# When a weight load is issued around a branch: attention, cosine routing and eight experts on one core

## The chip, the cores and the metric

The kernel runs on one core of a Trainium2 chip. A core has TensorE (PE, with PEld for its weight loads), VectorE (DVE), ScalarE (ACT), GpSimd (POOL) and SyncE (SP), each with its own stream of instructions; they meet through semaphores. Transfers are issued from the streams of SP and POOL and run on 16 DMA engines, which also bring the blocks of code that the engines execute. The metric is device microseconds of the core, median of three runs; lower is better.

## The reference

What is computed is an attention with a local window and a few global keys, and then a mixture of experts that gives each token to one expert:

```python
# attention: B=4, H=8, S=768, D=64; keys 0..7 and the last 96 are kept, with a bias by distance
a = exp(scores - max); a = a / (sum(a) + 1e-9); x = a @ v          # x: 3072 tokens of 512
# experts: E=8, F=1024
logits = unit(x) @ unit(expert_emb).T / tau
expert_idx = argmax(logits, axis=1)
gate_w = softmax(logits)[expert_idx]
for e in range(E):
    mask = expert_idx == e
    h = maximum(x[mask] @ w1[e], 0)
    out[mask] = gate_w[mask, None] * (h @ w2[e])
```

All is float32. The weights of one expert are two matrices of 2 MB.

## The kernel before

The first 200 us are the attention with the choice of expert; each token's row is written to DRAM and its number, row and gate go into a list by expert. The change lies in what follows: the loop over the eight experts at the end of the kernel's main function.

**How many tokens.** The number of tokens of an expert is known only on the chip. It is rounded up to a width of 128, 160, 192, ..., 512 (256 is the least from expert 1 on), and for every width there is an arm of code of its own. `tc.Switch` in `expert` lets TensorE, ScalarE and VectorE jump into the arm; each jumps for itself, and each jumps back to the common code behind the arms ("behind the choice") for itself. The register that names the arm is loaded by `take_width` (L1491, one load each on TensorE, ScalarE and VectorE) for the expert after the next, and `give_hint` (L1497) tells the engines' fetch of code which arm comes next. With this case's data the widths are 160, 320, 512, 320, 352, 384, 480 and 384.

**Inside an arm.** `first_by_seven` computes h of experts 1 to 7 as a 2x2 block product with seven products instead of eight (products at L1286). It needs sums of blocks of w1 and of x, made by VectorE ahead of time: `first_sums` (L1064 to L1067, tile fsum; two run in the arm of the expert before, two behind it) and `token_sums` (L1039 to L1042, tile xsum, split the same way). VectorE's additions of results are L1298, ScalarE's copies and relus L1312, L1317 and L1300. Then `part_in_arm` (L1232, eviction L1234) multiplies a last group of 64 rows, or 32, or both, by w2, and `second_in_arm` (L1219, eviction L1221) does whole tiles of 128 rows beyond the first 256. For width 320 there is one part of 64 rows and no tile; 352 has both parts; 480 both parts and a tile; 512 two tiles. Between products the next expert's rows are transposed (L1011) and copied (L1014).

**Behind the arm.** The first 256 rows go through class `Pair`, again a 2x2 block product of seven products (L1101), with four banks of PSUM. `begin` makes four of them: the first is copied by ScalarE (L1121, tile ptmp), the second is added to it by VectorE (L1105) and scaled by ScalarE (L1125), the third is added (L1105) and scaled (L1131), the fourth gives one part of y (L1112). `end` makes three more; the last of all waits until ScalarE has taken the product before it out of the same bank (L1144). What is left of the previous expert's pair (`unfinished`, L1112 or, behind expert 0, L1029) is done by VectorE first. In expert 0 the pair of another set of rows is finished by `end_apart`.

**What sets the order.** The order on TensorE, ScalarE, VectorE and POOL is that of the program text. In the common code behind the arm VectorE has: the width, the rest of y, two sums of x, two sums of w1, then the pair's additions. SP's stream in this part holds only loads of weights. `prepare(e + 1)` names POOL's gathers of rows (L985) and, from expert 2 on, `load_weights` for the next expert: w1 (L167), then w2 (L168), into the buffers that expert e - 1 used. Each load waits for the last reader of its buffer: for w1 these are TensorE's products in the arm and VectorE, for w2 the end of the pair. POOL scatters finished rows (L1238).

Of the kernel before, what the change touches and what calls it, by code (L numbers as in the profile page):

```python
# [12 lines left out]
ALU = mybir.AluOpType  # L13
# [7 lines left out]
P = 128  # L21
# [142 lines left out]

def load_weights(k, e, w):
    nc = k.nc
    nc.sync.dma_start(w[0][:], k.w1[e].rearrange("(c p) f -> p c f", p=P))  # L167
    nc.sync.dma_start(w[1][:], k.w2[e].rearrange("(f p) m -> p f m", p=P))  # L168


def load_weights_part(k, e, w, i):
# [822 lines left out]
def new_turned(k):  # L994
    return k.xtp.tile([P, k.NC, 2, CAP // 2], F32, name="xT", tag="xT")


def new_hidden(k):
    return k.hp.tile([P, k.NF, CAP], F32, name="hT", tag="hT")
# [7 lines left out]
def turn_row(k, rows, xT, j, copy):  # L1007

    ps = k.work.tile([P, k.NC, P], F32, name="work", tag="work")
    for c in range(k.NC):  # L1010
        k.nc.tensor.transpose(ps[:, c, :], rows[2][j][:, c * P : (c + 1) * P], k.ident[:])  # L1011
    half = P // 2
    for a in range(2):
        copy(out=xT[:, :, a, j * half : (j + 1) * half].rearrange("p c (q i) -> p c q i", i=LACE),  # L1014
             in_=laced(ps[:])[:, a])
# [30 lines left out]
def weight_sums(k, w2):  # L1046

    b = [[w2[:, 4 * i : 4 * i + 4, j * 256 : (j + 1) * 256] for j in range(2)] for i in range(2)]
    return right_sums(k, b, k.wsum)


def token_sums(k, xT):

    b = [[xT[:, 2 * i : 2 * i + 2, j] for j in range(2)] for i in range(2)]
    return right_sums(k, b, k.xsum, True)
# [20 lines left out]
def first_sums(k, w1):  # L1076
    return left_sums(k, first_weights(k, w1), k.fsum, True)


def hidden_sums(k, a):  # L1080
    return left_sums(k, a, k.hsum)


class Pair:
# [24 lines left out]

    def last(self, i, out, x, z):  # L1110

        self.k.nc.vector.scalar_tensor_tensor(out=out, in0=x, scalar=self.gate[i], in1=z, op0=ALU.mult, op1=ALU.add)  # L1112

    def scatter(self, i):
        return lambda: scatter_rows(self.k, self.y[i][:], self.ids[:, i, 1:2])

    def begin(self, split=False):
        nc, (t1, t2, t3, t4), (s1, s2, s3, s4) = self.k.nc, self.sums, self.left
        m = self.m = self.bank()
        self.product(m, self.a[0][0], self.b[0][0])  # L1120
        nc.scalar.copy(out=self.p1, in_=m)  # L1121
        n = self.bank()
        self.product(n, s2, t2)
        self.plus(self.u2, n, self.p1)
        nc.scalar.mul(self.u2g, self.u2, self.gate[0])  # L1125
        if split:
            self.fourth()
        n = self.bank()
        self.product(n, s3, t3)
        self.plus(self.u3, n, self.u2)  # L1130
        nc.scalar.mul(self.u3g, self.u3, self.gate[1])  # L1131
        n = self.bank()
        self.product(n, self.a[1][1], t4)
        self.last(1, self.part(1, 0), n, self.u3g)

    def fourth(self):
        self.product(self.m, self.a[0][1], self.b[1][0], True)
        self.k.nc.scalar.mul(self.part(0, 0), self.m, self.gate[0])
# [16 lines left out]
    def end_apart(self):  # L1155

        t1, (s1, s2, s3, s4) = self.sums[0], self.left
        n = self.bank()
        self.product(n, s1, t1)
        self.last(1, self.part(1, 1), n, self.u3g)  # L1160
        self.last(0, self.u3, n, self.u2g)
        n = self.bank()
        self.product(n, s4, self.b[1][1])
        self.last(0, self.part(0, 1), n, self.u3)
        return [self.scatter(0), self.scatter(1)]
# [49 lines left out]
def second_in_arm(k, t, hT, w2, j):  # L1215
    nc = k.nc
    ps = k.work.tile([P, k.DM], F32, name="work", tag="work")
    for i, f in enumerate(k.order):
        nc.tensor.matmul(ps[:], lhsT=hT[:, f, j * P : (j + 1) * P], rhs=w2[:, f, :],  # L1219
                         start=i == 0, stop=i == k.NF - 1)  # L1220
    nc.scalar.mul(t.y[:, j - 1, :], ps[:], t.rows[0][:, j, 2:3])  # L1221
# [27 lines left out]
def wait_for(k, i, others):  # L1249
    for x in others:  # L1250
        k.tc.add_manual_dep(i.ins, x.name,
                            mybir.DependencyInfo(mybir.DependencyClass.Sync, mybir.DependencyReason.DATA),
                            reason="it comes behind all of them")
# [75 lines left out]
def expert(k, now, coming, widths, unfinished):  # L1329


    tc = k.tc
    w1, w2 = now.w
    hT = new_hidden(k)
    if coming:
        coming.xT = new_turned(k)

    def between(f):
        at = {1: (0,), 2: (1,), 3: (2,), 4: (3,)} if now.e else {5: (0,), 6: (1, 2), 7: (3,)}
        for j in at.get(f, ()) if coming else ():  # L1340
            turn_row(k, coming.rows, coming.xT, j, k.nc.scalar.copy)

    a = [[hT[:, 4 * j : 4 * j + 4, i * P : (i + 1) * P] for j in range(2)] for i in range(2)]
    now.sums, spare = weight_sums(k, w2)
    left, making = hidden_sums(k, a)
    more, ahead = [], []
    if coming:
        coming.token_sums, more = token_sums(k, coming.xT)
        if now.e:
            coming.first_sums, ahead = first_sums(k, coming.w[0])  # L1350
    spare = [spare[:2], spare[2:], ahead[:1], ahead[1:2], more[:2], []]
    tiles = range(2 if now.e else 1, CAP // P)
    ps = None if now.e else k.work0.tile([P, k.DM], F32, name="work", tag="work")
    k.order = list(range(4, 8)) + list(range(4)) if now.e else list(range(8))
    steps = widths_of(now.e)
    for arm in tc.Switch(now.width.index, len(steps), hint=now.width.hint):
        w = steps[arm]
        if now.e:
            first_by_seven(k, now, hT, w, between, list(spare))
            for make in making:  # L1360
                make()
        else:
            first_by_eight(k, now.xT, w1, hT, w, between)
        for size in (64, 32):
            if w % (2 * size) >= size:
                part_in_arm(k, now, hT, w2, w // (2 * size) * 2 * size, size)
        for j in tiles:
            if j < w // P:
                second_in_arm(k, now, hT, w2, j)
        if ps:  # L1370
            second(k, ps, hT, w2, range(k.NF // 2))

    def scatters():
        for j in tiles:
            scatter_rows(k, now.y[:, j - 1, :], now.tile_ids[:, j : j + 1])
        for size in (64, 32):
            scatter_rows(k, now.y_part[size][:], now.parts[size][0], P // size)

    def choose_next():
        if coming:  # L1380
            give_hint(k, coming.e, widths[coming.e])
        if now.e + 2 < k.E:
            widths.append(take_width(k, now.e + 2))

    out = [scatters]
    if now.e:
        pair = Pair(k, now.rows, a, left, w2, now.sums)
        choose_next()
        out += unfinished.pop()()
        for make in more[2:] + ahead[2:]:  # L1390
            make()
        pair.begin()
        ps = k.work0.tile([P, k.DM], F32, name="work", tag="work")
        unfinished.append(pair.end(ps[:, 0:256]))
        out.append(pair.scatter(1))
    else:
        choose_next()
        out += unfinished.pop()()
        for make in more:
            make()  # L1400
        second(k, ps, hT, w2, range(k.NF // 2, k.NF))
        unfinished.append(lambda: end_second(k, now.rows, ps))
    return out


def widths_of(e):
    return WIDTHS[PAIR:] if e else WIDTHS
# [78 lines left out]
def take_width(k, e):  # L1486

    t = Net()
    n = len(widths_of(e))
    engines = ARMS if e else ARMS[:2]  # L1490
    v = k.nc.values_load(k.pick[0:1, e : e + 1], engines=engines, min_val=0, max_val=n - 1)  # L1491
    t.index, t.hint = {eng: v for eng in engines}, "expert%d" % e
    return t
# [74 lines left out]
def kernel(  # L1568
# [13 lines left out]
    n = Net()  # L1582
    n.tc, n.nc = tc, tc.nc
    nc = n.nc
# [24 lines left out]
    with ExitStack() as moe:  # L1609
# [43 lines left out]
        def prepare(e):  # L1653
            t = Net()
            t.e = e
            t.y, t.y_part = ys[e % 2]
            xgs, t.gathers = gather_rows(n, n.ids[:, e], n.xgp)
            t.rows = n.mt[:, e], n.ids[:, e], xgs
            if e < 2:
                t.w = n.w[e]  # L1660
            else:
                t.w = new_weights(n, (wp_a, n.wp_b)[e % 2])
                load_weights(n, e, t.w)
            return t

        with tc.manual_schedule(engines=ORDERED | set(ARMS) | {mybir.EngineType.Pool}):
# [20 lines left out]
            widths = [take_width(n, 0), take_width(n, 1)]  # L1687
            give_hint(n, 0, widths[0])
            pair = Pair(n, n.first.rows, a, left, n.w[0][1], sums)
# [10 lines left out]
            first, making = first_sums(n, n.w[1][0])  # L1700
# [3 lines left out]
            for e in range(n.E):  # L1704
                now, coming = coming, None
# [44 lines left out]
```

## Time and profile before

| What | us |
| --- | --- |
| Median of the three runs (530.98 to 533.39) | 532.84 |
| The profiled execution's own time | 532.6 |
| Its span, from the first to the last instruction | 530.9 |
| TensorE busy in the span | 502.7 |
| VectorE, ScalarE, POOL busy | 302.2, 197.5, 148.3 |
| From the first product of expert 1's arm to the end of expert 7's pair | 234.3 to 523.5 |

| Expert | Width | Arm and pair, us | w1 for the next expert but one issued at | w2 issued at |
| --- | --- | --- | --- | --- |
| 0 | 160 | 208.8 to 234.3 | 222.95 | 234.31 |
| 1 | 320 | 234.3 to 271.0 | 253.19 | 269.14 |
| 2 | 512 | 271.0 to 324.9 | 305.80 | 324.93 |
| 3 | 320 | 324.9 to 359.5 | 343.79 | 359.58 |
| 4 | 352 | 359.5 to 397.7 | 383.12 | 397.72 |
| 5 | 384 | 397.7 to 436.8 | 417.68 | 436.86 |
| 6 | 480 | 436.8 to 486.1 | none | none |
| 7 | 384 | 486.1 to 523.5 | none | none |

A line of the order of time gives the start in us, the length, the engine, the line of the kernel, the operation, the tiles, and in brackets the idle time before it with what ended it. "Issue" there means that the profile shows nothing that the engine waited for; fetching code is such a case. A line can stand for several instructions in a row. Matmul ends are modelled. Times of TensorE's and VectorE's jumps, of packets and of the clock are from records of the same trace.

### The profile page before, as it was taken

Reading aid. Unit: us, or ns where it says so; the run is one execution under the profiler, and the core shown is the slowest. Engines: PE = TensorE matmul, PEld = TensorE weight load, DVE = VectorE, ACT = ScalarE, POOL = GpSimd, SP = SyncE. Lnnn points to the kernel's source line nnn. Section 1 sums busy time; section 2 is a strip of 40 time slices with the busy share of each in tenths; the row PEclk is TensorE's granted clock in tenths of the full one; section 3 lists DMA queues with packets and bytes.
Section 4 is the critical chain, followed back from the end, with each engine's and each line's share of the span. In section 5 each row is a group of like instructions: output and inputs, shape, how many; then the busy total and the mean of one; then the engine's idle time right before and its main releaser. Section 6 shows DMA issues by size and latency. Waiting matters only on the chain.

```text
span 530.9 us, 13718 instructions
## 1 busy us (share of the span) xinstructions
PE 502.7 (95%) x5606; PEld 412.8 (78%) x5606; DVE 302.2 (57%) x601; ACT 197.5 (37%) x494; POOL 148.3 (28%) x169
## 2 busy tenths in 40 slices
PE   8999999999989998999979999989999999999994
PEld 7677787877766687779758669979789789869963
DVE  5756767756686664848535624745646554733531
ACT  4966766766644311304022312312312222312210
POOL 4221121242364335342330024033042050012032
PEclk9999999999998999999989999999999999999998
DMA  9999999998333527875560055257057424001001
GB/s 172 199 199 183 225 227 196 200 206 213 106 92 101 136 47 187 238 248 177 190 236 26 2 200 187 98 189 260 10 206 239 156 69 159 1 24 58 0 22 67
DMA packets 111421, 76.32 MB, mean 144 GB/s; under 512 B 87077, under 2 KB 95269, under 8 KB 111281
## 3 DMA queue, kind: packets, MB, share of 16 engines
q1 hardware_dynamic: 102769, 59.00, 42.2%
q0 software_dynamic: 6912, 15.26, 8.9%
q8 instruction: 63, 1.03, 0.9%
q14 instruction: 77, 0.63, 0.4%
q10 hardware_dynamic: 1600, 0.39, 0.3%
HBM read 61.66 MB, written 17.16 MB: 148 GB/s over the span
## 4 chain that ended last, share of the span: by engine, by line
PE 75%; issue 8%; DVE 6%; ACT 4%; POOL 3%; DMA 3%; POOLq 0%; DVEq 0%; ACTq 0%
PE big L1286 23%; PE big L1101 9%; PE work L1219 7%; PE od L508 6%; PE pa L479 5%; PE work L1101 4%; PE pa L454 3%; PE od L518 3%; PE pa L670 3%; PE work L1232 3%; PE work L1011 2%; ACT ex L485 2%; PE big L1262 2%; PE pa L581 2%; PE work L1021 1%
## 5 line engine op out<-in xcount | busy, mean ns | idle before, releaser
L492 DVE TENSOR_TENSOR ex<-ex,table 126x768 f32<-126x768 f32 x64 | 59.9, 941 | 42.5 <-ACT ex L485 42.1
L1298 DVE TENSOR_TENSOR hT<-big,hT 128x320 f32<-128x320 f32 (+4 forms) x70 | 39.5, 566 | 49.6 <-PE big L1286 42.2
L1238 POOL DMA_INDIRECT out_dram<-y_arm,tids x17 | 17.5, 1031 | 168.7 <-ACT y_arm L1221 122.8
L1286 PE MATMUL big<-xT,w1t 128*128 128x160 f32 (+4 forms) x336 | 61.1, 336 | 1.9 <-issue 1.9
L485 ACT ACTIVATE ex<-pa 126x384 f32<-126x384 f32 (+1 forms) x128 | 53.2, 476 | 19.8 <-PE pa L479 18.9
L1286 PEld LDWEIGHTS big<-xT,w1t 128*128 128x128 f32 x336 | 55.4, 194 | 5.2 <-issue 2.8
L508 PE MATMUL od<-ex,v 126*64 126x192 f32 (+1 forms) x576 | 47.4, 310 | 0.1
L985 POOL DMA_INDIRECT xg<-x_dram,idss x32 | 32.5, 1014 | 44.9 <-PE big L1286 18.5
L508 PEld LDWEIGHTS od<-ex,v 126*64 126x64 f32 x576 | 35.2, 138 | 8.2 <-issue 3.7
L479 PE MATMUL pa<-qT,kT 64*32 64x128 f32 (+3 forms) x2048 | 39.6, 265 | 1.5 <-issue 1.3
L479 PEld LDWEIGHTS pa<-qT,kT 64*32 64x32 f32 (+1 forms) x2048 | 30.1, 106 | 13.7 <-issue 9.2
L1286 PE MATMUL big<-xsum,fsum 128*128 128x160 f32 (+4 forms) x224 | 39.6, 330 | 0.0
L1014 ACT COPY xT<-work 128x256 f32<-128x256 f32 x56 | 18.1, 375 | 56.1 <-PE work L1011 53.1
L256 POOL DMA_INDIRECT meta<-mt,slot x24 | 27.0, 1123 | 39.0 <-DVE rd L552 20.2
L1286 PEld LDWEIGHTS big<-xsum,fsum 128*128 128x128 f32 x224 | 36.1, 190 | 1.1
L1219 PE MATMUL work<-w2t,hT 128*128 128x512 f32 x80 | 35.1, 593 | 0.0
L429 POOL COPY v<-v 30x896 f32<-30x896 f32 (+1 forms) x15 | 17.9, 1207 | 53.8 <-DMA v<-in_v_dram 27.1
L1101 PE MATMUL big<-wsum,hsum 128*128 128x256 f32 x136 | 31.1, 380 | 0.9 <-ACT ptmp L1121 0.5
L1300 ACT ACTIVATE hT<-hT 128x320 f32<-128x320 f32 (+4 forms) x42 | 21.7, 533 | 25.0 <-DVE hT L1298 24.9
L1101 PEld LDWEIGHTS big<-wsum,hsum 128*128 128x128 f32 x136 | 25.7, 190 | 5.5 <-issue 1.2
L1101 PE MATMUL big<-w2t,hT 128*128 128x256 f32 x112 | 27.7, 385 | 1.7 <-ACT y L1234 1.1
L1219 PEld LDWEIGHTS work<-w2t,hT 128*128 128x128 f32 x80 | 15.1, 190 | 17.5 <-issue 17.2
(245 smaller groups left out, 880.3 us busy)
## 6 DMA issues: line engine op xcount, KB each, us to landing
w1t<-in_moe_w_dram SPq DMA_DIRECT2D x6, 2048.0 KB
w2t<-in_moe_w_dram SPq DMA_DIRECT2D x6, 2048.0 KB
v<-in_v_dram SPq DMA_DIRECT2D x32, 192.0 KB
x_dram<-xs SPq DMA_DIRECT2D x23, 256.0 KB
k<-in_k_dram SPq DMA_DIRECT2D x28, 192.0 KB
q<-in_q_dram SPq DMA_DIRECT2D x28, 192.0 KB
w1t<-in_moe_w_dram SPq DMA_DIRECT2D x32, 128.0 KB
w2t<-in_moe_w_dram SPq DMA_DIRECT2D x32, 128.0 KB
```

Source lines behind the costliest of these rows:

```text
L256: i = nc.gpsimd.indirect_dma_start(out=k.meta[:], out_offset=bass.IndirectOffsetOnAxis(ap=slot[:, t : t + 1], axis=0), in_=mt[:, t, :], in ...
L479: i = nc.tensor.matmul(u.sp[e][k0:k1, a * n + c0 : a * n + c1], lhsT=t.kT[rows, j, k0:k1], rhs=t.qT[rows, j * BLK + c0 : j * BLK + c1], st ...
L485: nc.scalar.activation(u.ex[:, e], u.sp[e][0:ROWS, 0 : 2 * u.n].rearrange("p (a c) -> p a c", a=2), AF.Exp, scale=k.scale)
L492: nc.vector.tensor_tensor(out=exv, in0=exv, in1=tab[:, :, 0 : u.n // BLK, :], op=ALU.mult)
L508: nc.tensor.matmul(g.od[a][e * D : (e + 1) * D, at : at + c1 - c0], lhsT=g.v[0:ROWS, 2 * a + e, u.j, :], rhs=u.ex[:, e, a, c0:c1], start=f ...
L985: i = k.nc.gpsimd.indirect_dma_start(out=xg[:], out_offset=None, in_=k.x_dram[0 : upto or k.N + 1, :], in_offset=bass.IndirectOffsetOnAxis ...
L1014: copy(out=xT[:, :, a, j * half : (j + 1) * half].rearrange("p c (q i) -> p c q i", i=LACE), in_=laced(ps[:])[:, a])
L1101: self.k.nc.tensor.matmul(ps, lhsT=x[:, f, :], rhs=w[:, f, :], start=f == 0 and not add, stop=True, skip_group_check=True)
L1219: nc.tensor.matmul(ps[:], lhsT=hT[:, f, j * P : (j + 1) * P], rhs=w2[:, f, :], start=i == 0, stop=i == k.NF - 1)
L1286: nc.tensor.matmul(to[f // 2][:, f % 2 * 256 : f % 2 * 256 + h], lhsT=x[:, l, f * P : (f + 1) * P], rhs=y[:, l, 0:h], start=not (add or f ...
L1298: nc.vector.tensor_tensor(out=to, in0=x, in1=z, op=ALU.add)
L1300: nc.scalar.activation(to, to, AF.Relu)
```

## The change

Four edits stand in one diff:

- `load_weights` returns its first load (w1), and `prepare` makes it wait for an instruction called `out_again`: ScalarE's copy of the pair's first product (L1121), in expert 0 VectorE's first result in `end_apart` (L1112). Both stand behind the arm of the expert whose buffer is loaded anew. Each takes the place of the wait for TensorE's products in the arm.
- The two sums of x and the two sums of w1 that VectorE had ahead of the pair move into `Pair.begin`: the sums of x behind the first addition, one sum of w1 behind the second, the other behind the result y.
- `take_width` moves out of `choose_next` to the place behind the second addition, ahead of the sum of w1 there; for expert 0 it stays behind the hint.
- In an arm with both parts the one of 32 rows comes ahead of the one of 64.

In the instruction streams the counts of products, sums and transfers stay the same. On TensorE the register load stands behind the third product of the pair instead of ahead of the first. On POOL and SP one thing more moves: in expert 1, POOL's four gathers now stand ahead of its jump, and so does SP's load of w2 for expert 2.

```diff
 def load_weights(k, e, w):
     nc = k.nc
-    nc.sync.dma_start(w[0][:], k.w1[e].rearrange("(c p) f -> p c f", p=P))
+    first = nc.sync.dma_start(w[0][:], k.w1[e].rearrange("(c p) f -> p c f", p=P))
     nc.sync.dma_start(w[1][:], k.w2[e].rearrange("(f p) m -> p f m", p=P))
+    return first
...
-    def begin(self, split=False):
+    def begin(self, split=False, spare=((), (), ())):
+
+        def fill(i):
+            for make in spare[i]:
+                make()
+
         nc, (t1, t2, t3, t4), (s1, s2, s3, s4) = self.k.nc, self.sums, self.left
         m = self.m = self.bank()
         self.product(m, self.a[0][0], self.b[0][0])
-        nc.scalar.copy(out=self.p1, in_=m)
+        self.k.out_again = nc.scalar.copy(out=self.p1, in_=m).ins
         n = self.bank()
         self.product(n, s2, t2)
         self.plus(self.u2, n, self.p1)
         nc.scalar.mul(self.u2g, self.u2, self.gate[0])
+        fill(0)
         if split:
             self.fourth()
         n = self.bank()
         self.product(n, s3, t3)
         self.plus(self.u3, n, self.u2)
         nc.scalar.mul(self.u3g, self.u3, self.gate[1])
+        fill(1)
         n = self.bank()
         self.product(n, self.a[1][1], t4)
         self.last(1, self.part(1, 0), n, self.u3g)
+        fill(2)
...
     def end_apart(self):
...
-        self.last(1, self.part(1, 1), n, self.u3g)
+        self.k.out_again = self.last(1, self.part(1, 1), n, self.u3g).ins
...
-        for size in (64, 32):
+        for size in (32, 64):
             if w % (2 * size) >= size:
                 part_in_arm(k, now, hT, w2, w // (2 * size) * 2 * size, size)
...
     def choose_next():
         if coming:
             give_hint(k, coming.e, widths[coming.e])
-        if now.e + 2 < k.E:
-            widths.append(take_width(k, now.e + 2))
...
         choose_next()
         out += unfinished.pop()()
-        for make in more[2:] + ahead[2:]:
-            make()
-        pair.begin()
+        number = [lambda: widths.append(take_width(k, now.e + 2))] if now.e + 2 < k.E else []
+        pair.begin(spare=(more[2:], number + ahead[2:3], ahead[3:]))
...
     else:
         choose_next()
+        widths.append(take_width(k, 2))
         out += unfinished.pop()()
...
                 t.w = new_weights(n, (wp_a, n.wp_b)[e % 2])
-                load_weights(n, e, t.w)
+                wait_for(n, load_weights(n, e, t.w), [n.out_again])
```

More of the change, by code (lines that the diff above doesn't have):

```diff
@@ L1110, in last @@
     def last(self, i, out, x, z):
-        self.k.nc.vector.scalar_tensor_tensor(out=out, in0=x, scalar=self.gate[i], in1=z, op0=ALU.mult, op1=ALU.add)
+        return self.k.nc.vector.scalar_tensor_tensor(out=out, in0=x, scalar=self.gate[i], in1=z, op0=ALU.mult, op1=ALU.add)
     def scatter(self, i):
         return lambda: scatter_rows(self.k, self.y[i][:], self.ids[:, i, 1:2])
-    def begin(self, split=False):
+    def begin(self, split=False, spare=((), (), ())):
+        def fill(i):
+            for make in spare[i]:
+                make()
         nc, (t1, t2, t3, t4), (s1, s2, s3, s4) = self.k.nc, self.sums, self.left
```

## The prediction, made before the changed kernel ran

> **What bounds the kernel now.** First the page: TensorE is busy 95% of the span and carries the chain of work that ended last.
>
> ```profile
> PE 502.7 (95%) x5606; PEld 412.8 (78%) x5606; DVE 302.2 (57%) x601; ACT 197.5 (37%) x494; POOL 148.3 (28%) x169
> ...
> PE 75%; issue 8%; DVE 6%; ACT 4%; POOL 3%; DMA 3%; POOLq 0%; DVEq 0%; ACTq 0%
> ```
>
> So only a stage in which TensorE stands still can give anything. I cut the expert part into stages, one for each expert (from the first product of its arm to that of the next), and asked for busy time in each; the column after the stretch is its length, then PE's busy time.
>
> ```profile
> core 0: us, PE busy (x) PEld busy (x) DVE busy (x) ACT busy (x) POOL busy (x), PEclk, DMA share, GB/s
> 234.30:271.00 36.70, 33.10 (x216) 29.39 (x215) 22.13 (x32) 9.29 (x24) 10.12 (x10) 1.00 0.52 174
> ...
> 324.90:359.50 34.60, 33.08 (x218) 29.73 (x217) 21.26 (x31) 9.30 (x24) 10.83 (x10) 1.00 0.47 168
> 359.50:397.70 38.20, 36.49 (x283) 33.01 (x282) 21.95 (x31) 10.17 (x25) 10.70 (x10) 1.00 0.48 164
> ```
>
> Experts 1, 3 and 4 leave TensorE idle for 3.60, 1.52 and 1.71 us; in the stages of experts 2, 5, 6 and 7 the two columns agree within 0.05 us. The whole change therefore plays for about 7 us, plus what hides in the clock. The order of time for expert 1, in which the fetch of code is seen only as idle time ("issue"):
>
> ```profile
> 253.19 0.37 SPq L167 DMA_DIRECT2D w1t<-in_moe_w_dram  x1
> 260.69 0.75 DVE L1029 TENSOR_SCALAR y<-work,mts 128x512 f32<-128x512 f32 x1 [5.63 <-issue]
> 261.11 0.37 ACT L1121 COPY ptmp<-big 128x256 f32<-128x256 f32 x1 [5.69 <-PE big L1101]
> 265.21 0.94 DVE L1105 TENSOR_TENSOR ptmp<-big,ptmp 128x256 f32<-128x256 f32 x2
> 267.12 1.99 PE L1101 MATMUL work<-w2t,hsum 128*128 128x256 f32 x8 [1.70 <-ACT ptmp L1144]
> 271.05 2.30 PE L1286 MATMUL big<-xT,w1t 128*128 128x256 f32 x5 [1.94 <-issue]
> ```
>
> VectorE and ScalarE end the arm near 255 and do nothing for 5.6 us, although TensorE had the first product of the pair ready near 256.4. VectorE then works through y, two sums of x and two of w1 before its first addition of the pair (265.21), so ScalarE's copy at L1144 comes at 266.61 and the last product waits 1.70 us. Then the jump into expert 2's arm costs 1.94 us. The other stages:
>
> ```profile
> 237.19 1.22 DVE L1039 TENSOR_TENSOR wsum<-w2t 128x1024 f32<-128x1024 f32 x1 [3.04 <-issue]
> ...
> 351.39 0.48 DVE L1112 SCALAR_TENSOR_TENSOR y<-work,mts,u2g 128x256 f32<-128x256 f32 x1 [5.71 <-DMA out_dram<-y_arm,tids]
> 357.55 1.99 PE L1101 MATMUL work<-w2t,hsum 128*128 128x256 f32 x8 [1.52 <-ACT ptmp L1144]
> ...
> 384.57 1.32 PE L1101 MATMUL big<-w2t,hT 128*128 128x256 f32 x5 [1.07 <-ACT y L1234]
> 386.52 0.81 PE L1101 MATMUL big<-w2t,hT 128*128 128x256 f32 x3 [0.64 <-issue]
> ...
> 468.20 0.48 DVE L1112 SCALAR_TENSOR_TENSOR y<-work,mts,u2g 128x256 f32<-128x256 f32 x1 [2.83 <-issue]
> ```
>
> Expert 6, where no weights load any more, shows what leaving an arm costs VectorE alone: 2.83 us. With the w1 load just issued it is 5.63 and 5.71 (and 5.82 in expert 5, where 7 us of tile products cover it). So the load adds about 2.8 us to a fetch of code.
>
> **The load of w1 behind the choice.** It removes the 2.8 us from the exits. A rule that speaks against this stands in the Trainium skill, "Runtime: NRT & Kernel Launch", Instruction fetch mechanics: a taken branch to code outside the two blocks held forces a fetch whatever else runs. The 2.83 us of expert 6 agree that a rest stays; 5.63 against 2.83 says that the load doubles it, on which the page is silent. By the rule alone this part is worth nothing, by the rows 2.8 us on each of two engines. ScalarE then copies the first product of expert 1's pair at 258.1 (exit 255.4 plus 2.7), not 261.1. SP, with nothing in its queue but w1 and then w2, issues w1 at 258.3 instead of 253.2, and in the other stages some 4 to 9 us later too. A 2 MB load takes about 8 us from issue to its last packet (packets of 254.24 to 261.18 for the issue at 253.19), and w1 is first read halfway through the next arm (288.3 for this one), so no reader is late; w2 follows at the end of the pair as before.
>
> **The sums among the additions, the width later.** On VectorE 0.69+0.68 us (x) and 1.22+1.23 us (w1) leave the place ahead of the first addition; the register load costs about 0.45 us each on VectorE and ScalarE and 0.70 on TensorE's sequencer, and moves behind the third product. There TensorE's queue holds products, ScalarE waits over 2 us for L1144, and VectorE has 1.2 us between additions: hidden. Check on expert 2, whose pair runs without a stall: first addition to 316.8, two sums of x to 318.1, second addition to 318.6, width and one sum of w1 to 320.1, y to 320.6, the last sum to 321.8, and the addition behind L1144 starts at 322.0 as now. It fits with 0.2 us left; without that cover the next arm's VectorE start would slip by as much.
> For expert 1 either of these two parts is enough: with the exit still late at 261.1, additions without the 3.8 us of sums ahead still have L1144 done at 264.3, before TensorE wants it at 265.0. So 1.70 and 1.52 us go in experts 1 and 3. TensorE's 0.39 us between the 64-row part and the pair (weight loads 254.39 to 254.78, the same in expert 3) goes too, as its sequencer saves 0.70. Together 1.70+0.39+1.52+0.39 = 4.0 us.
>
> **The 32-row part first.** Only experts 4 and 6 take both parts here. In expert 4 the branch comes only 0.8 us before the array runs dry, against 1.85 in expert 1 where a 64-row part stands last; 1 us of lead and the 0.70 us above exceed the gap of 1.07. The 0.64 us inside the product is a block of code fetched at 383.70 beside the load issued at 383.12; that load now starts about 4 us later. Against it ScalarE's last eviction is 0.47 us, not 0.37: 0.1, hidden as TensorE doesn't wait for it in expert 1. Gain 1.71, at least 0.7 (the width alone).
>
> **What the later load hits instead.** (a) Expert 1's entry. The load for expert 2 now waits for VectorE's L1112 (229.64), so it and w2 behind it fill the engines from 230.8 past 240, and VectorE jumps into arm 1 at 234.07. Before, the load was over at 231.7. The nearest row is the exit: plus 2.6 us. VectorE's 237.19 becomes 239.8, its two sums of w2 end at 242.1, its first addition at 242.6, and TensorE wants that at 241.5: a loss of 1.1 us (0 if the fetch slips in early, 1.8 with a longer one). (b) Expert 2's entry. TensorE's branch there took 3.38 us in the trace, and 4.34 at the entry of expert 1 beside a load. Decoded at 264.35 (L1144 done at 264.0), 2.15 us before the array runs dry at 266.5, it leaves 1.23 to 2.2 us idle, now 1.94. (c) Later entries: VectorE may be 0.6 to 2 us late, but there it starts only 0.2 us behind TensorE instead of 2.9, so 2 us are free.
>
> The clock hangs on (b). Expert 2's first 32 matmuls take longer than later ones of the same form:
>
> ```profile
> 271.05 8.83 PE big L1286 x32
> ...
> 291.99 6.91 PE big L1286 x32
> ```
>
> The trace has half the clock granted from 271.23 to 274.64: 1.9 us lost. The skill's "TensorE: Matmul & The Clock Gate" (section "Why this matters for your kernels") sets the danger at idle gaps over about 3 us; by that a gap of 1.94 costs nothing more and the removal of stalls gains none. Here 1.94 us did cost it (with 1.70 just before), 1.52 in expert 3 did not. By the row, a gap of 1.2 would save all 1.9, one of 2.2 nothing. I take the middle: 1.7 idle and half the penalty, 2.65 in place of 3.85, gain 1.2 (from -0.3 to +2.6).
>
> POOL's gathers, which now stand ahead of its jump in expert 1, start about 5 us sooner and add to (a); nobody waits for them in this stage.
>
> **Sum.** 4.0 + 1.7 + 1.2 - 1.1 = 5.8 us. The profiled execution took 532.6 with a span of 530.9; its span becomes 525.1. It lies 0.2 below the median of the three runs, 532.84, so I forecast 532.84 - 5.8 = 527.0.
>
> **The rivals.**
> 1. The load isn't what holds the exits (their 5.6 us would stay). For: the line of expert 3 names a scatter. Against: 2.83 without a load. The order of the additions alone still gives 4.0 + 0.7, and no loss at the entry: about 528.1.
> 2. The fetches move with the load: expert 1's entry loses 1.8, expert 2's gap grows to 2.2 plus 0.6 with the full clock penalty (-0.9), expert 4 keeps its 0.64, and VectorE's later entries eat about 1 us in two stages. 4.0 + 1.1 - 1.8 - 0.9 - 2.0 = 0.4: about 532.4, no change. For: ScalarE, VectorE and TensorE all jump within the 8 us of the later load. Against: the slack in (c).
> 3. Slower. TensorE's branches into arms 3 to 6 now take 0.3 to 0.4 us because the block was fetched ahead, at 314.7, 350.7, 390.5 and 426.4. If the later load holds these fetches until the jump, each entry costs 3.4 to 4.3 less 2.15 of lead, about 1.7 us; it decides where the block arrives later than 2 us before the arm's first product. Four such gaps and the half clock behind two (1.9 each) are 10.6 us: 532.84 - 5.8 + 10.6 = 537.6. Against: on the new times those fetches come 1 to 2 us ahead of the load.
>
> **How the numbers follow.** The main case 0.50 (its own range 525 to 529), rival 1 0.20, rival 2 0.20, rival 3 0.10. A measurement of this kernel can't tell less than about 0.5% (2.7 us) from no change. Faster: the first two nearly whole and about a quarter of rival 2, 0.74; same 0.17; slower 0.09. The low end 523.5 adds the full clock gain and no loss at the entry; the high end 531.5 takes in half of rival 2.
>
> **What would show it.** Right: VectorE's and ScalarE's idle time at the exits of experts 1, 3 near 2.8; no wait for L1144; no 1.07 and 0.64 in expert 4; w1 issued behind L1121. Wrong: new waits of TensorE for L1298 in arm 1 beyond 1.8 us; idle "issue" of TensorE at entries 3 to 6; half clock at a new place; a wait for w1t at L1064.

## The result and the profile after

| | before | after |
| --- | --- | --- |
| Median, us (13 runs each) | 531.61 | 527.88 |
| Lowest and highest | 527.83 to 533.39 | 523.08 to 532.87 |
| Profiled execution, its span | 532.6, 530.9 | 523.84, 522.0 |

The ratio of the times is 0.9929 with a 95% interval of 0.99 to 0.9959: the change gains 3.8 us (2.2 to 5.3), where 5.8 were forecast. Ratios here leave out executions that a throttled clock made much longer (one of from_three took 577.63 us at a mean granted clock of 0.85, one of after_again 845.06 us at 0.56).

The profiled execution of after is 4 us under its own median. Its 8.9 us of span less come in three pieces: 1.83 before expert 0's arm starts, in code that the change doesn't touch (that start lies anywhere from 203.1 to 208.8 us in the profiles of this case), 1.57 in expert 0, and 5.50 in experts 1 to 7. Only the last is compared below. The page of after, busy time and shares of the chain that ended last:

```profile
PE 498.9 (96%) x5606; PEld 411.8 (79%) x5606; DVE 301.8 (58%) x601; ACT 197.5 (38%) x494; POOL 152.5 (29%) x169
...
PE 56%; issue 2%; DVE 1%; DMA 1%; POOLq 0%; POOL 0%; DVEq 0%
```

The chain of after is followed back only to about 201 us, so its shares add up to 60%. TensorE bounds it as before. Busy time by stage in after, experts 1 to 4 (columns as in the prediction: stretch, its length, PE's busy time):

```profile
core 0: us, PE busy (x) PEld busy (x) DVE busy (x) ACT busy (x) POOL busy (x), PEclk, DMA share, GB/s
230.70:267.39 36.69, 33.31 (x217) 29.71 (x216) 22.00 (x33) 9.45 (x24) 12.67 (x11) 1.00 0.63 214
267.39:319.56 52.17, 52.17 (x218) 39.72 (x219) 22.88 (x31) 12.02 (x25) 10.80 (x10) 1.00 0.34 119
319.56:352.42 32.86, 32.86 (x219) 29.85 (x218) 21.33 (x31) 9.50 (x24) 11.06 (x10) 1.00 0.53 183
352.42:388.66 36.24, 36.24 (x282) 32.97 (x282) 21.77 (x31) 10.13 (x25) 12.47 (x10) 1.00 0.48 167
```

Experts 3 and 4 no longer leave TensorE idle at all (1.52 and 1.71 us before). Expert 1 still leaves 3.38 us idle, against 3.60. Expert 2 is shorter although it had no idle time to lose. The order of time shows why:

```profile
236.63 1.23 DVE L1040 TENSOR_TENSOR wsum<-w2t 128x1024 f32<-128x1024 f32 x1 [5.86 <-issue]
239.45 2.44 PE L1295 MATMUL big<-xsum,fsum 128*128 128x160 f32 x16 [1.17 <-DVE hT L1307]
255.73 0.75 DVE L1030 TENSOR_SCALAR y<-work,mts 128x512 f32<-128x512 f32 x1 [2.63 <-issue]
256.13 0.37 ACT L1127 COPY ptmp<-big 128x256 f32<-128x256 f32 x1 [2.67 <-issue]
256.53 0.37 SPq L167 DMA_DIRECT2D w1t<-in_moe_w_dram  x1
...
263.29 1.89 PE L1102 MATMUL work<-w2t,hsum 128*128 128x256 f32 x8
267.39 1.97 PE L1295 MATMUL big<-xT,w1t 128*128 128x256 f32 x8 [2.21 <-issue]
...
342.94 0.48 DVE L1113 SCALAR_TENSOR_TENSOR y<-work,mts,u2g 128x256 f32<-128x256 f32 x1 [2.59 <-DMA out_dram<-y_arm,tids]
```

The exits are what the prediction said: 2.63 and 2.67 us at expert 1, 2.59 at expert 3, in place of 5.63, 5.69 and 5.71; w1 is issued behind ScalarE's copy (256.13, now L1127); and the last product of the pair (263.29) waits for nothing. But VectorE enters arm 1 after 5.86 us, not 3.04, TensorE stands still for 1.17 us behind it, and the jump into expert 2's arm costs 2.21 us, not 1.94. What expert 2 gained is in the chain of after:

```profile
267.39 7.15 PE big L1295 x32
```

These 32 products took 8.83 us in before, with half the clock granted for 3.41 us. In this execution of after no half clock was granted in the expert part.

### The profile page after: what moved, and what is told of

Same layout as the page of the kernel before. It is cut to its first block, busy times and chain, and to the rows that moved or that the text cites. A ratio compares the mean times of both kernels' runs of the same rounds, so it can differ in the third digit from the quotient of the medians.

```text
span 522.0 us, 13699 instructions
## 1 busy us (share of the span) xinstructions
PE 498.9 (96%) x5606; PEld 411.8 (79%) x5606; DVE 301.8 (58%) x601; ACT 197.5 (38%) x494; POOL 152.5 (29%) x169
## 4 chain that ended last, share of the span: by engine, by line
PE 56%; issue 2%; DVE 1%; DMA 1%; POOLq 0%; POOL 0%; DVEq 0%
PE big L1295 24%; PE big L1102 12%; PE work L1228 7%; PE work L1102 5%; PE work L1241 4%; PE work L1012 2%; PE big L1271 2%; DMA xg<-x_dram,idss 1%; PE work L1022 1%; POOL xg L986 0%; POOLq L1722 0%; DVE wsum L1041 0%; DVE y L1113 0%; DVE xsum L1042 0%; DVE xT L1041 0%
## 5 line engine op out<-in xcount | busy, mean ns | idle before, releaser
L1295 PE MATMUL big<-xT,w1t 128*128 128x160 f32 (+4 forms) x336 | 59.4, 330 | 2.2 <-issue 2.2
L1295 PEld LDWEIGHTS big<-xT,w1t 128*128 128x128 f32 x336 | 54.2, 190 | 4.9 <-issue 3.1
L986 POOL DMA_INDIRECT xg<-x_dram,idss x32 | 36.6, 1143 | 49.3 <-PE work L1012 15.9
L480 PEld LDWEIGHTS pa<-qT,kT 64*32 64x32 f32 (+1 forms) x2048 | 30.1, 106 | 14.5 <-issue 10.9
L430 POOL COPY v<-v 30x896 f32<-30x896 f32 (+1 forms) x15 | 16.5, 1111 | 53.2 <-DMA v<-in_v_dram 29.8
L1106 DVE TENSOR_TENSOR ptmp<-big,ptmp 128x256 f32<-128x256 f32 x16 | 6.8, 422 | 37.6 <-ACT ptmp L1127 17.0
```

Source lines behind the costliest of these rows:

```text
L480: i = nc.tensor.matmul(u.sp[e][k0:k1, a * n + c0 : a * n + c1], lhsT=t.kT[rows, j, k0:k1], rhs=t.qT[rows, j * BLK + c0 : j * BLK + c1], st ...
L986: i = k.nc.gpsimd.indirect_dma_start(out=xg[:], out_offset=None, in_=k.x_dram[0 : upto or k.N + 1, :], in_offset=bass.IndirectOffsetOnAxis ...
L1295: nc.tensor.matmul(to[f // 2][:, f % 2 * 256 : f % 2 * 256 + h], lhsT=x[:, l, f * P : (f + 1) * P], rhs=y[:, l, 0:h], start=not (add or f ...
```

## The experiments

The stages of all kernels, from their profiles (us from the first product of an arm to that of the next; expert 7 to the end of its pair). The last columns are TensorE's larger idle times in experts 1 to 4, and whether expert 2 began at half the clock. Idle time ahead of arm 1's first product counts in e0 and is named only from 0.5 us on (1.12 in from_three, 0.66 in no_wait_again; it is 0.43 in no_wait and 0.33 in nw_parts). Expert 5 took 39.14 and expert 7 37.55 in every one.

| Kernel | e0 | e1 | e2 | e3 | e4 | e6 | e1 to e7 | idle | half clock |
| --- | --- | --- | --- | --- | --- | --- | --- | --- | --- |
| before | 25.28 | 36.93 | 53.69 | 34.64 | 38.14 | 49.26 | 289.36 | 1.70, 1.94, 1.52, 1.07, 0.64 | yes |
| after | 23.71 | 36.67 | 52.01 | 32.86 | 36.24 | 49.40 | 283.86 | 1.17, 2.21 | no |
| after_again | 23.68 | 37.43 | 53.69 | 32.86 | 36.24 | 49.40 | 286.30 | 1.66, 2.48 | yes |
| no_wait | 24.10 | 34.38 | 52.01 | 32.86 | 36.24 | 49.40 | 281.58 | 1.28 | no |
| from_three | 24.59 | 35.47 | 52.01 | 32.86 | 36.53 | 49.40 | 282.95 | 1.12, 2.37 | no |
| wait_only | 23.43 | 37.13 | 53.69 | 32.86 | 37.67 | 49.26 | 287.30 | 1.18, 2.66, 1.01, 0.23 | yes |
| nw_sums | 23.82 | 36.92 | 53.69 | 34.10 | 36.43 | 49.40 | 287.22 | 1.48, 2.15, 0.97 | yes |
| nw_width | 24.03 | 34.46 | 52.01 | 32.86 | 36.24 | 49.40 | 281.65 | 1.36 | no |
| nw_parts | 24.26 | 35.03 | 52.01 | 32.86 | 37.71 | 49.26 | 283.55 | 1.93, 0.37, 0.80 | no |
| sixth_sooner | 23.48 | 34.17 | 52.01 | 33.65 | 36.42 | 49.40 | 282.35 | 0.82, 0.53 | no |
| apart | 23.51 | 32.86 | 51.99 | 32.86 | 36.24 | 49.40 | 280.03 | none | no |
| no_wait_again | 24.03 | 34.49 | 52.01 | 32.86 | 36.25 | 49.41 | 281.70 | 0.66, 1.40 | no |

Each row is one profiled execution; what each kernel changes stands with its edit below. Four of them, no_wait, after_again, from_three and wait_only, ran on one chip beside the same runs of before (526.53 us).

**The later load, the one part that was meant to free the exits, taken out again** (the run is called no_wait).

```diff
-                wait_for(n, load_weights(n, e, t.w), [n.out_again])
+                load_weights(n, e, t.w)
```

> The changed kernel with w1 loaded as before (as soon as TensorE is done with the buffer), everything else of the change kept. If the order of the additions covers the late exits by itself: VectorE and ScalarE leave the arms of experts 1 and 3 after 5.6 us again, but no wait of TensorE for the copy behind the sixth product; the wait of 1.17 us in arm 1 is gone, the gap ahead of arm 2 is 1.3 to 1.6 us instead of 2.2, and expert 4 gets back 0.64 us at most: 1 to 2.5 us faster than the changed kernel, near 526. If the later load is what carries the change: 2 to 4 us slower than the changed kernel, near 531.

Measured over five rounds: 518.34 us, ratio 0.9855 (0.9824 to 0.9887). The changed kernel itself, run beside it:

> The changed kernel once more, beside the three others. 527.9, ratio 0.993. A second profile of it: TensorE's gap ahead of arm 2 again near 2.2 us, in which the half clock falls in most executions (1.7 us); a wait of 1.2 us for the first addition in arm 1.

522.52 us, ratio 0.9918 (0.9894 to 0.9942). The intervals don't meet: without the wait the kernel is 4.2 us faster than with it by the medians, 3.3 us by the ratios. The stages of no_wait for experts 1 and 3 (header as above), and its order of time around expert 1's exit:

```profile
227.57:261.95 34.38, 33.10 (x216) 29.76 (x217) 21.81 (x32) 9.39 (x24) 10.72 (x10) 1.00 0.53 176
...
313.96:346.82 32.86, 32.86 (x217) 29.84 (x216) 21.08 (x31) 9.50 (x24) 10.09 (x10) 1.00 0.52 178
```

```profile
229.60 1.23 DVE L1040 TENSOR_TENSOR wsum<-w2t 128x1024 f32<-128x1024 f32 x1 [2.59 <-issue]
253.83 0.75 DVE L1030 TENSOR_SCALAR y<-work,mts 128x512 f32<-128x512 f32 x1 [5.23 <-issue]
254.52 0.37 ACT L1127 COPY ptmp<-big 128x256 f32<-128x256 f32 x1 [5.56 <-PE big L1102]
254.93 0.42 DVE L1106 TENSOR_TENSOR ptmp<-big,ptmp 128x256 f32<-128x256 f32 x1 [0.35 <-ACT ptmp L1127]
257.46 0.46 ACT L1153 ACTIVATE ptmp<-work,mts 128x256 f32<-128x256 f32 x1
258.78 1.89 PE L1102 MATMUL work<-w2t,hsum 128*128 128x256 f32 x8
261.96 2.40 PE L1295 MATMUL big<-xT,w1t 128*128 128x256 f32 x10 [1.28 <-issue]
```

The exits are late again (5.23 and 5.56 us), and it doesn't matter: VectorE's first addition follows ScalarE's copy at once, since no sums stand ahead of it, and the copy out of the bank (L1153) ends at 257.92, 0.9 us before TensorE wants it. Expert 3 is as short as with the wait. What the wait did cost is gone: VectorE enters arm 1 after 2.59 us, and the gap ahead of arm 2 falls to 1.28.

**The wait for the loads of experts 3 to 7 alone**, so that expert 2's weights load as before:

```diff
-                wait_for(n, load_weights(n, e, t.w), [n.out_again])
+                first = load_weights(n, e, t.w)
+                if e > 2:
+                    wait_for(n, first, [n.out_again])
```

> The changed kernel, but the load of w1 for expert 2 goes out as before; the loads for experts 3 to 7 wait as changed. If that one load is what delays VectorE's entry into arm 1: its idle time there falls from 5.86 to about 3 us, TensorE's wait of 1.17 us for the first addition goes, and the rest stays as it is: 1.2 us faster than the changed kernel, near 526.7. If the entry is late for another reason (the code, or the gathers moved ahead): no difference, near 527.9.

521.22 us, ratio 0.991 (0.9879 to 0.9941): between the two, and told apart from neither. Its order of time:

```profile
229.06 2.41 PE L1295 MATMUL big<-xT,w1t 128*128 128x160 f32 x16 [1.12 <-issue]
230.55 1.23 DVE L1040 TENSOR_TENSOR wsum<-w2t 128x1024 f32<-128x1024 f32 x1 [2.75 <-issue]
264.52 3.69 PE L1295 MATMUL big<-xT,w1t 128*128 128x256 f32 x16 [2.37 <-DVE wsum L1040]
```

VectorE's entry into arm 1 is back at 2.75. Without the wait, POOL's gathers and SP's load of w2 for expert 2 also go back behind their jumps here, as in no_wait, so this run moves more than one load. The trace of after rules the gathers out: they start at 239.10 there, behind VectorE's first instruction in the arm (236.63). TensorE's own jump there, beside the early load, left 1.12 us of idle time (0.66 in no_wait_again, 0.43 in no_wait, 0.33 in nw_parts, nothing over 0.2 in nw_sums, nw_width, sixth_sooner and apart). So at arm 1 the early load can have a price too, up to 1.12 us, against 1.17 to 1.66 with the wait. The 2.37 at arm 2 stays, because the load for expert 3 is still the later one: that gap belongs to the wait at expert 1's pair.

**The wait alone**, in the kernel before:

```diff
-                load_weights(n, e, t.w)
+                wait_for(n, load_weights(n, e, t.w), [n.out_again])
```

> The kernel before with only the later load of w1. Exits of experts 1 and 3 at 2.8 us, so the first addition of expert 1's pair comes about 4 us earlier than before even behind the four sums, and no wait for the copy is left (1.7 and 1.5 us gained); the 0.64 us in expert 4 go, the 1.07 stay; arm 1 loses 1.2 to 1.6 us and the gap ahead of arm 2 is 2 us or more. About 2 us faster than before, near 529.5. If it takes no part in the gain: as before, 531.6, or 1.5 us slower for the loss in arm 1.

524.14 us, ratio 0.998 (0.9952 to 1.0008): no difference that can be told. In order of time:

```profile
236.11 2.44 PE L1287 MATMUL big<-xsum,fsum 128*128 128x160 f32 x16 [1.18 <-DVE hT L1299]
252.79 0.75 DVE L1030 TENSOR_SCALAR y<-work,mts 128x512 f32<-128x512 f32 x1 [3.03 <-issue]
264.50 2.13 PE L1287 MATMUL big<-xT,w1t 128*128 128x256 f32 x7 [2.66 <-issue]
376.17 1.32 PE L1102 MATMUL big<-w2t,hT 128*128 128x256 f32 x5 [1.01 <-ACT y L1235]
377.72 0.81 PE L1102 MATMUL big<-w2t,hT 128*128 128x256 f32 x3 [0.23 <-issue]
```

The exit is freed (3.03) and the copy is waited for in neither expert 1 nor 3; in expert 3 that is worth the whole 1.78 us. In expert 1 it is given back, 1.18 us in the arm and 2.66 at the next jump. In expert 4 the 0.64 inside the product fell to 0.23, but 1.01 ahead of it stayed.

**The three other parts, each undone in no_wait** (one profiled execution each).

The sums ahead of the pair again:

```diff
-        pair.begin(spare=(more[2:], number + ahead[2:3], ahead[3:]))
+        for make in more[2:] + ahead[2:]:
+            make()
+        pair.begin(spare=((), number, ()))
```

> no_wait with the two sums of x and the two of w1 ahead of the pair again. The exits of experts 1 and 3 are late (5.8 us), so with 3.8 us of sums ahead of the first addition TensorE's wait for the copy comes back: about 1.3 us in expert 1 and 1.1 in expert 3 (1.70 and 1.52 less the width's 0.45), stages of experts 1 and 3 longer by that, the others as in no_wait. If the width's move alone had freed the pair: no wait.

527.28 us, against 529.2 for before on that chip. In order of time:

```profile
261.74 0.95 DVE L1106 TENSOR_TENSOR ptmp<-big,ptmp 128x256 f32<-128x256 f32 x2
263.65 1.99 PE L1102 MATMUL work<-w2t,hsum 128*128 128x256 f32 x8 [1.48 <-ACT ptmp L1153]
267.79 2.78 PE L1295 MATMUL big<-xT,w1t 128*128 128x256 f32 x7 [2.15 <-issue]
```

The wait for the copy is back, in expert 3 too (0.97), the gap at arm 2 grows to 2.15, and the half clock falls on it again. The place of the sums is worth 281.58 against 287.22, 5.6 us; it is the larger part of what no_wait gains. Of the 5.6 us, 1.68 are the half clock, which a gap of this length brought in some profiles and not in others.

The width ahead of the pair again:

```diff
+        if now.e + 2 < k.E:
+            widths.append(take_width(k, now.e + 2))
...
-        pair.begin(spare=(more[2:], number + ahead[2:3], ahead[3:]))
+        pair.begin(spare=(more[2:], ahead[2:3], ahead[3:]))
```

> no_wait with the register load for the width ahead of the pair again. TensorE's sequence behind the arm is 0.70 us longer: 0.3 to 0.4 us more in the stages of experts 1 and 3, in expert 4 0.6 us or less if the 64-row part gives the lead; no wait for the copy (the additions still stand ahead of the sums). If expert 4's second gap of 0.64 us comes back with it, that gap was the width's and not the load's.

519.53 us; the stages of experts 1 to 7 sum to 281.65, against 281.58 and 281.70 in the two profiles of no_wait. With the 32-row part first, moving the width is worth nothing that these profiles show.

The part of 64 rows first again:

```diff
-        for size in (32, 64):
+        for size in (64, 32):
```

> no_wait with the part of 64 rows ahead of that of 32 again. Only experts 4 and 6 take both. Expert 4: 1.07 less the width's 0.70, so 0.3 to 0.4 us of gap ahead of its pair, and perhaps the 0.64 us inside the first product; expert 6 the same as in no_wait or 0.14 us shorter, as in the kernel before (49.26 against 49.40).

521.36 us. In order of time, expert 4:

```profile
372.18 0.37 SPq L167 DMA_DIRECT2D w1t<-in_moe_w_dram  x1
372.93 1.75 PE L1102 MATMUL big<-w2t,hT 128*128 128x256 f32 x7 [0.37 <-PE work L1241]
375.47 0.48 PE L1102 MATMUL big<-w2t,hT 128*128 128x256 f32 x1 [0.80 <-issue]
```

Expert 4 takes 37.71 instead of 36.24: the order of the parts is worth 1.47 us there and costs 0.14 in expert 6 (49.26 against 49.40). The gap ahead of expert 4's pair is 0.37 us where before had 1.07. That is the 0.70 expected of the width; no run moves the width alone with the 64-row part first, so its share is not shown.

Expert 1 takes one part only and is the same code as in no_wait, and yet its stage is 0.65 us longer, because the gap ahead of arm 2 is longer:

```profile
263.58 3.69 PE L1295 MATMUL big<-xT,w1t 128*128 128x256 f32 x16 [1.93 <-issue]
```

TensorE's jump took 4.05 us here, 3.43 in no_wait, with no load of w1 beside either (it ended at 255.80, the jump began at 259.27). One profile of this gap is thus good to some 0.6 us only.

**Is the gap that is left, 1.28 us ahead of arm 2, the last wait on ScalarE's copy?** TensorE's sequencer reads its instructions ahead of the array; in no_wait it comes to its jump at 258.26, right behind the end of the copy (257.92) that the last product has to wait for. Two edits of no_wait free it. The sixth product moved forward, behind the third:

```diff
     def begin(...):
         fill(1)
+        if ps is not None:
+            self.product(ps, s1, t1)
+            nc.scalar.mul(self.p5, ps, self.gate[1])
+            self.plus(self.part(1, 1), self.p5, self.u3g)
...
     def end(self, ps):
-        self.product(ps, s1, t1)
-        nc.scalar.mul(self.p5, ps, self.gate[1])
-        self.plus(self.part(1, 1), self.p5, self.u3g)
```

> no_wait, with the pair's product that ScalarE has to copy before the last one (s1 times t1) one place earlier, ahead of the product of the fourth place. If the gap ahead of arm 2 is the time of TensorE's jump (3.5 us) less the lead that this copy leaves it (2.2 us): the copy comes 1.73 us sooner, the lead grows to 3.9, and the gap of 1.28 us is gone: stage of expert 1 33.1 us instead of 34.4, 1.3 us faster than no_wait, ratio near 0.983. If TensorE's queue doesn't run further ahead, or the jump waits for the array: the gap stays.

521.07 us over five rounds, ratio 0.9872 (0.9839 to 0.9906). In order of time:

```profile
255.45 0.75 DVE L1030 TENSOR_SCALAR y<-work,mts 128x512 f32<-128x512 f32 x1 [5.19 <-issue]
256.25 2.00 PE L1102 MATMUL work<-wsum,hsum 128*128 128x256 f32 x8 [0.82 <-DVE y L1030]
263.41 3.69 PE L1296 MATMUL big<-xT,w1t 128*128 128x256 f32 x16
...
342.06 2.00 PE L1102 MATMUL work<-wsum,hsum 128*128 128x256 f32 x8 [0.53 <-DVE y L1113]
```

The jump into arm 2 (263.41) costs nothing, but the product that moved forward now waits for the bank of PSUM that the late VectorE has yet to read, in experts 1 and 3: the late exit is on the path again. The other edit leaves the order and gives the sixth product another bank, from which VectorE reads it directly:

```diff
-        self.product(ps, s1, t1)
-        nc.scalar.mul(self.p5, ps, self.gate[1])
-        self.plus(self.part(1, 1), self.p5, self.u3g)
+        n = self.k.work.tile([P, self.k.DM], F32, name="work", tag="work")[:, 0:256]
+        self.product(n, s1, t1)
+        self.last(1, self.part(1, 1), n, self.u3g)
+        self.last(0, self.u2g, n, self.u2g)
         self.fourth()
-        self.product(ps, s4, self.b[1][1], True)
+        self.product(ps, s4, self.b[1][1])
```

> no_wait, with the last product of the pair in a bank of its own: VectorE takes the product before it straight from its bank (gate times it, added to the two sums), ScalarE's copy of it falls away, and TensorE's last product waits for nothing recent. If the gap ahead of arm 2 is TensorE's jump less its lead, and the new waits in sixth_sooner came only from the bank that VectorE's late exit holds: no gap ahead of arm 2, no new one in experts 1 and 3, stage of expert 1 33.1 us instead of 34.4, the others as in no_wait, 1.3 us faster than no_wait. If the bank of the last product is still held by VectorE: a gap of up to 1 us comes in experts 1 and 3 and nothing is won.

The stages of experts 1 to 4 in apart:

```profile
226.62:259.48 32.86, 32.86 (x218) 29.71 (x216) 21.61 (x33) 9.04 (x23) 10.51 (x11) 1.00 0.54 183
259.48:311.47 51.99, 51.99 (x218) 39.54 (x218) 24.22 (x33) 11.55 (x24) 11.85 (x11) 1.00 0.37 129
311.47:344.33 32.86, 32.86 (x218) 29.85 (x217) 21.33 (x32) 9.04 (x23) 10.06 (x10) 1.00 0.49 176
344.33:380.57 36.24, 36.24 (x282) 32.97 (x281) 21.89 (x32) 9.70 (x24) 9.22 (x10) 1.00 0.48 167
```

TensorE is never idle there. Its time over five rounds is 518.5 us, ratio 0.9855 (0.9828 to 0.9883), beside no_wait again:

> no_wait once more, beside apart on the same chip: ratio 0.986, stages of experts 1 to 7 281.6 us in all.

518.49 us, 0.9853 (0.9828 to 0.9877). The stages of experts 1 to 7 are 1.67 us shorter in apart's profile (280.03 against 281.70), and the medians are equal. A spread of several us from run to run lies in the attention ahead of this part; whether it, or a half clock in the executions that were not profiled, takes the 1.67 is open. What is shown is that the gap is gone, not that the kernel is faster for it. By their ratios both beat the changed kernel.

## Why the prediction was right, and where it was wrong

By its own terms, for the profiled execution of after; the second profile of the same kernel in brackets:

| Step | forecast | measured |
| --- | --- | --- |
| Expert 3, wait for the copy and the 0.39 | -1.91 | -1.78 [-1.78] |
| Expert 4, parts and width | -1.71 | -1.90 [-1.90] |
| Expert 1: copy and 0.39, less the late VectorE and the jump at its end (1.7 for 1.94) | -1.2 | -0.26 [+0.50] |
| Expert 2, half clock | -0.95 | -1.68 [0] |
| Expert 6 | 0 | +0.14 [+0.14] |
| Sum | -5.8 | -5.5 [-3.1] |

**The total** of 527.0 stands against 527.88. The stages explain -5.5 or -3.1 us, by whether expert 2's start meets the half clock, and the 3.8 us gained lie between. How often it does so in the executions without a profile isn't recorded: only their mean clock is, and the half clock also falls in the attention and at the end. That the total is as near as 0.9 us is in part luck. The base of the forecast, 532.84, was the median of three runs; from the 531.61 of all thirteen the same gain would have given 525.8. And in the first profile expert 1 gave 0.9 us less than forecast, but expert 2, where no half clock fell, 0.7 more.

**Right.** The load does hold the exits: VectorE's at expert 1 took 2.6 to 3.0 us in the profiles with the later load, 5.2 to 5.7 in those with it early, so rival 1 (the load isn't what holds them) is false. In expert 1's arm VectorE comes 2.8 us later than before, and the loss is 1.17 [1.66] where 1.1 was forecast. POOL's gathers take no part in it: they do not start 5 us sooner, as the prediction had it, but 8.4 us behind the arm's first product, where before has 5.8. The entries of arms 3 to 6 have no gap on TensorE, so what rival 3 feared, that the later load would hold back their code, did not come. VectorE was 0.5 to 1.7 us late there (3.2 to 4.4 us, 2.7 before), and nothing waited for it, as (c) had said. In experts 1 and 3 either of the two parts is enough against the wait for the copy: wait_only and no_wait each have none.

**Wrong: "It removes the 2.8 us from the exits", counted as a part of the gain.** The exits are sooner, but once the sums are moved, nothing on the path that sets the end becomes so: in no_wait expert 3 is the same 1.78 us shorter, and expert 4 the same 1.90, without the later load. The prediction had said that either part is enough, and rival 1 had given the order alone 4.7 us, but with the gap ahead of arm 2 and its half clock left where they were. There it failed: without the wait for the copy TensorE reaches its branch sooner, and with the early load it jumps in 3.43 us, so the gap is 1.28 (1.36, 1.40 and, with the long jump, 1.93 in three other profiles), and no half clock fell in any of the four. The change without the later load gives 7.6 to 8.2 us. The gap is the time of the jump less TensorE's lead, the time from its branch to the end of its last product ahead, plus about 0.25 us:

| Profile | w1 load | lead | jump | gap |
| --- | --- | --- | --- | --- |
| before | early | 1.70 | 3.38 | 1.94 |
| nw_sums | early | 1.71 | 3.59 | 2.15 |
| no_wait | early | 2.41 | 3.43 | 1.28 |
| nw_parts | early | 2.38 | 4.05 | 1.93 |
| after | later | 2.61 | 4.55 | 2.21 |
| apart | early | 3.76 | 3.32 | none |

The wait for the copy costs 0.7 us of lead (nw_sums against no_wait), the later load about 1.1 us of jump. What lengthened the jump of nw_parts is open.

**Wrong in size: step (b), "1.7 idle and half the penalty".** It was 2.21, 2.48, 2.37 and 2.66 with the wait, at or past the upper bound of 2.2. TensorE's jump into arm 2 took 4.55 us in after and 4.70 to 4.81 in the three others; the lead was 2.6 where 2.15 had been taken. In after w1 is issued 10.9 us ahead of arm 2's first product (256.53, 267.39), in before 17.9 us ahead (253.19, 271.05); its packets end at 264.45, so they reach into the jump (262.57 to 267.12). The middle was taken between 3.38 and 4.34; the row beside a load was the nearer one. The whole penalty of the half clock is 1.68 us by the length of the stage, not the 1.9 that the prediction read from the row.

**Wrong: "TensorE's 0.39 us ... goes too, as its sequencer saves 0.70".** It was never idle time of the products: it is a pause of the weight loads (PEld), which stays, and the 64-row part of expert 3 and its first pair product start 3.61 us apart both times. Before, then after:

```profile
341.80 3.67 PE L1232 MATMUL work<-w2t,hT 128*64 128x256 f32 x32
345.41 1.59 PEld L1101 LDWEIGHTS big<-w2t,hT 128*128 128x128 f32 x8 [0.39 <-issue]
345.41 1.99 PE L1101 MATMUL big<-w2t,hT 128*128 128x256 f32 x8
...
336.46 3.67 PE L1241 MATMUL work<-w2t,hT 128*64 128x256 f32 x32
340.06 1.59 PEld L1102 LDWEIGHTS big<-w2t,hT 128*128 128x128 f32 x8 [0.38 <-issue]
340.07 1.99 PE L1102 MATMUL big<-w2t,hT 128*128 128x256 f32 x8
```

nw_width says the same. That the sum for expert 3 was still near is because the wait for the copy cost 1.78 us by the length of the stage, not the 1.52 that the row shows; the ends of matmuls are modelled, and the idle time before the next is short by as much.

**Half right: the 0.64 us in expert 4 as a block "fetched at 383.70 beside the load".** With the 64-row part first the load does matter: 0.64 and 0.80 with it early, 0.23 with it late (wait_only). But with the 32-row part first the gap is gone even with the early load (no_wait). So what removes it in after is the order of the parts, for which the prediction gave the lead of TensorE's sequencer. "At least 0.7 (the width alone)" is half right: with the 64-row part first the gap ahead of the pair falls from 1.07 to 0.37 (nw_parts), but the stage only from 38.14 to 37.71; with the 32-row part first the width gives nothing (nw_width).

**Not foreseen:** expert 0's stage is 25.28 us in before's profile and 23.4 to 24.6 in all others, wait_only among them. The traces place it: in before expert 0's part of 32 rows takes 3.62 us, from 219.45 to 223.07, with gaps between its products, against 1.88 in wait_only and 2.22 in after. This lies ahead of everything that the change moves, so 1.4 of the 1.57 us that after saves in expert 0 are no gain of the change. Only one profile of before was taken; why it paused there is open.

## What to carry to other kernels

When an engine arrives late because its jump shares the transfers with a bulk load, first ask what its lateness holds up: putting the work that others wait for ahead of the work that nobody waits for took the late exits off the path here (5.6 us by the stages, the half clock included), while delaying the load only moved it beside the next jumps. A delayed transfer has to be followed to the end: list the jumps in the 8 us after its new start, not only those that it left. And where the last instruction ahead of a jump waits for a buffer, the sequencer's lead over the array is cut short (1.7 to 2.4 us here); a second buffer gives it back (3.8 us in apart).

## What the runs showed of the hardware

- VectorE's jumps into and out of the arms left it idle for 2.1 to 3.2 us with no load beside them, 3.2 to 4.7 where a load of 2 MB had been issued some 6 to 7 us before, and 5.1 to 6.4 with one issued 1 to 4 us before. The difference moves with the load.
- TensorE's jump into arm 2 took 3.3 to 4.05 us in eight profiles and 4.5 to 4.8 in the four where w1's packets reached into it; into arm 1, 3.3 to 3.9 with the later load and 4.3 to 6.3 with the early one. But a load isn't all that lengthens a jump: at the end of the program, where no weights load and three engines jump together, TensorE's took 4.2 to 4.5.
- Idle time of 2 to 2.7 us can bring half the clock, but doesn't always. Ahead of expert 2 it came after gaps of 1.94, 2.15, 2.48 and 2.66 us, not after 1.93, 2.21 and 2.37, and never after 1.40 or less. The gaps of 1.94 and 2.15 had another wait, of 1.70 and 1.48 us, only 2 us ahead of them; the lowest that brought it alone is 2.48. It then costs the stage 1.68 us. The Trainium skill's "TensorE: Matmul & The Clock Gate" ("Why this matters for your kernels") puts the danger above about 3 us; by these runs it begins somewhat lower, though the rows show idle time of TensorE about 0.25 us short.
- For TensorE's idle time the length of the stage is the safer measure: by it the waits of 1.52 and 1.71 us in experts 3 and 4 were 1.78 and 1.90.
